# A two-row reload of x on ScalarE's DMA queue, behind the gate's exponential

## The chip, the cores and the metric

The kernel runs on one core of one Trainium2 chip. The metric is the device time of one execution in microseconds, median of several runs. The median before is 137.99 us over three runs (137.84 to 138.12).

## The reference

One decoding step of a transformer block for four tokens (B = 4, D = 1024): grouped-query attention with 32 query heads over 4 key/value heads and a window of the last 2048 cached positions, then a gated feed-forward layer of width 3584. All inputs are bf16.

```python
def _A_ref(x, k_cache, v_cache, wq, wo):
    W = min(4096, max(256, Sk // 4))          # 2048 of 8192 positions
    q = (x @ wq).reshape(B, Sq, Hq, Dh).transpose(0, 2, 1, 3)
    k = jnp.repeat(k_cache[:, :, Sk - W:, :], rep, axis=1)
    v = jnp.repeat(v_cache[:, :, Sk - W:, :], rep, axis=1)
    p = _softmax(jnp.einsum("bhqd,bhkd->bhqk", q, k) * (Dh ** -0.5), axis=-1)
    o = jnp.einsum("bhqk,bhkd->bhqd", p, v)
    return o.transpose(0, 2, 1, 3).reshape(B, Sq, Hq * Dh) @ wo

def _B_ref(x, w1, w3, w2):
    h = _silu(x @ w1) * (x @ w3)
    return h @ w2

h = x + _A_ref(_layernorm(x), A_k_cache, A_v_cache, A_wq, A_wo)
h2 = h + _B_ref(_layernorm(h), B_w1, B_w3, B_w2)      # the output
```

## The kernel before

Some 55.6 MB of weights and cache are read once, and nearly all of the arithmetic is matrix products of a few rows, so the kernel is built around one stream of loads. SyncE (SP) issues it, in the order of the list `plan`, into a ring of SBUF (`ring`, five regions reused in turn): wq in two pieces with two small side loads, k, v, wo, w1, w3, and w2 in four pieces (17, 7, 3 and 1 of its 28 row groups, called w2a to w2d here). `load_next` issues the next entry of the list, and a piece that overwrites a part of the ring waits for the matmuls that read it. All these loads share one DMA queue (q1 in the profile).

ScalarE's own DMA queue (q10) carries three transfers only: two loads at the start that bring x into `x_sb` (L158, four rows of 512 columns each), and the store of the output at the end (L515, sixteen rows of 256 columns). A second copy of x in another layout, `x_q`, comes through SP's queue (L169). `x_sb` is read by the first layernorm alone (L180 and L187) in the first ten microseconds; the tile is kept, and nothing reads it later.

The work after attention goes in stages: `y_ps` (wo, L411), the second layernorm (L424 to L449), `gate_up("w1", g_ps)` on TensorE (L459), and then the gate's SiLU. Of that, ScalarE computes the exponential `eg` (L471), and VectorE adds 1, takes the reciprocal and multiplies by the gate (L472 to L475) while w3 is still arriving. Then `gate_up("w3", u_ps)`, the product `hg` (L478), a transpose, and the `down` products with w2 (L492). VectorE and ScalarE each copy half of the result (L513, L514), and ScalarE issues the store (L515).

Order around the change. The framework puts instructions of each engine in a fixed order and draws the waits itself. Transfers issued by SP and ScalarE get one of eight completion semaphores, in turn in the order of issue, and a transfer first waits until the former user of its semaphore has landed. The kernel before has 24 such transfers, exactly three rounds of eight: the third round is wo, w1, w3, w2a, w2b, w2c, w2d and the store, so the store has the eighth semaphore. At the end of the program (all of it at L541) SP waits for all of these semaphores and for the other engines, with two semaphores per wait instruction, in this order: third and fourth; second and fifth; first and sixth; seventh and VectorE's; eighth and ScalarE's. Then the engines meet at barriers, and the program ends.

`tc.issue_after(ins)` orders what is issued inside its block behind `ins` on the same engine; it does not make it wait until `ins` has finished.

Of the kernel before, what the change touches and what calls it, by code (L numbers as in the profile page):

```python
# [11 lines left out]
ACT = mybir.ActivationFunctionType  # L12
# [7 lines left out]
def kernel(  # L20
# [13 lines left out]
    nc = tc.nc  # L34
# [14 lines left out]
    x_flat = A_x.flatten_outer_dims()  # L49
# [19 lines left out]
    CG = D // JG  # L69
    CF = F // JG  # L70
    HF = CF // 2
# [84 lines left out]
    x_sb = act.tile([B, D], BF16)  # L156
# [11 lines left out]
    for c in range(2):  # L168
        nc.sync.dma_start(  # L169
            out=x_q[c * 2 * QD : (c + 1) * 2 * QD : RS, :],  # L170
            in_=x_flat.rearrange("b (j c) -> j b c", j=JG)[2 * c : 2 * c + 2],
# [7 lines left out]
    for c in range(2):  # L179
# [8 lines left out]
        out=xn[:], in0=x_sb[:], scalar1=mv[:, 0:1], scalar2=rstd[:, 0:1],  # L188
# [14 lines left out]
    for r0, ne, ns in SETS:  # L203
# [3 lines left out]
            out=xs[:, len(sl) : len(sl) + ns, : ne * 4].rearrange("b l (i s) -> b l i s", s=4),  # L207
            in_=v[:, KC - 1, :, :, :],
        )
        for l in range(ns):  # L210
            nc.tensor.transpose(
                out=ts_ps[: ne * 4, len(sl), :], in_=xs[:, len(sl), : ne * 4], identity=ident[:B, :B]
# [4 lines left out]
    for _, ne, ns in SETS:  # L217
# [14 lines left out]
        out=perm[:].rearrange("p (h dq) -> p h dq", dq=JG),  # L232
        in_=ident[:].rearrange("p (dq h) -> p h dq", dq=JG),
# [12 lines left out]
    for j in range(2, JG):  # L246
        nc.vector.tensor_tensor(
            out=same[:, 0, :], in0=same[:, 0, :], in1=ident[:, j * QD : (j + 1) * QD], op=ALU.add
# [35 lines left out]
    for r in range(REP):  # L284
        nc.tensor.transpose(out=qt_ps[:, r, :], in_=q_sb[:, r * Dh : (r + 1) * Dh], identity=ident[:])
    nc.vector.tensor_copy(
        out=qz[:, :, : Hkv * QD].rearrange("p b (g z) -> p b g z", g=Hkv)[:, :, :, :REP],
        in_=qt_ps[:].rearrange("p r (g x) -> p x g r", g=Hkv)[:, :B, :, :],
# [24 lines left out]
    for u, (b, n) in enumerate(units):  # L313
        k_v = loaded["k"][b]
        kT = ktpool.tile([P, NJ, P], BF16, tag="kT")
        for t in range(NJ // TB):
            kt_ps = psA.tile([P, TB, P], BF16, tag=f"kt{nt % 4}")
            for jj in range(TB):
                nc.tensor.transpose(  # L319
                    out=kt_ps[:, jj, :], in_=k_v[:, n * NJ + t * TB + jj, :], identity=ident[:]  # L320
# [21 lines left out]
        out=Pm[:], in_=scores_ps[:], func=ACT.Exp, bias=nmax[:], scale=1.0, accum_out=rsum[:]  # L342
# [6 lines left out]
    for c in range(NSB):  # L349
# [4 lines left out]
        for g in range(Hkv):  # L354
            if g % 2 == 0:
                nc.vector.tensor_scalar(  # L356
                    out=z[:, :, g, :], in0=pt_ps[:], scalar1=mask[:, g : g + 1], scalar2=None, op0=ALU.mult
# [10 lines left out]
        out=Dm[:], in0=ident[:].rearrange("p (g b r) -> p b g r", g=Hkv, b=B),  # L368
# [38 lines left out]
    g_ps = psB.tile([P, 2, 512], FP32, tag="g")  # L407
    u_ps = psB.tile([P, 2, 512], FP32, tag="u")
    for i in range(IO):
# [34 lines left out]
        out=hn[:], in0=h1[:], scalar1=tot[:, 0:1], scalar2=rstd2[:, 0:1],  # L444
# [5 lines left out]
        out=hnT[:].rearrange("p k x -> p (k x)"), in_=hn[:].rearrange("q (c k) -> q k c", k=KC)  # L450
# [3 lines left out]
    def gate_up(kind, out_ps):  # L454
# [13 lines left out]

    gate_up("w1", g_ps)
    eg = wide.tile([P, 2, HF], FP32, tag="w4k")  # L470
    nc.scalar.activation(out=eg[:], in_=g_ps[:, :, :HF], func=ACT.Exp, scale=-1.0)  # L471
    nc.vector.tensor_scalar_add(out=eg[:], in0=eg[:], scalar1=1.0)  # L472
    nc.vector.reciprocal(out=eg[:], in_=eg[:])  # L473
    gs = wide.tile([P, 2, HF], FP32, tag="w4k")
# [7 lines left out]
        out=hgT[:].rearrange("p i x -> p (i x)"),  # L482
        in_=hg[:].rearrange("q s c -> q (s c)").rearrange("q (c i) -> q i c", i=IF),
# [62 lines left out]
```

## Time and profile before

| | |
|---|---|
| median of the runs | 137.99 us (137.84 to 138.12) |
| profiled execution | span 136.0 us from its first to its last instruction; the page gives no other time of it, and the median is 1.99 us above the span |
| busy: PE, DVE, ACT | 72.3, 43.9, 31.0 us |
| DMA queue q1 (SP's loads) | 2604 packets, 55.58 MB, 95.6% of the 16 DMA engines' time |
| DMA queue q10 (ScalarE's) | 36 packets, 0.02 MB, 0.0% |
| mean TensorE clock granted | 0.720 |

The span counts from the first to the last instruction of the program. Issue times of transfers are times of the issuing engine's sequencer; the data moves later, and its landing is told by the completion semaphore. In views of the profile, "SPq" and "ACTq" are the sequencers of SP and ScalarE. Times with three decimals are start times of single records of the trace, in microseconds from the span's start.

### The profile page before, as it was taken

To read this page: it belongs to the slowest core of one execution; us is meant where nothing else is said; L and a number is where in the kernel's file an instruction comes from. 1 tells how busy PE (TensorE), PEld (TensorE's weight loads), DVE (VectorE), ACT (ScalarE), POOL (GpSimd) and SP (SyncE) were. 2 spreads that over 40 slices of the span, in tenths; PEclk is the share of its full clock that TensorE was granted. 3 is DMA by queue.
4 is the path that set the end of the run, shared out by engine and by line. 5 is a ranking of instruction groups with operands and counts; after the bars stand their busy time and mean duration, and the time that the engine had idled before them with its cause. 6 is when DMAs were issued, how large, how long until landed. Compare 5 with 4: busy or idle time off the path is not lost.

```text
span 136.0 us, 2436 instructions
## 1 busy us (share of the span) xinstructions
PE 72.3 (53%) x1096; PEld 46.1 (34%) x1096; DVE 43.9 (32%) x79; ACT 31.0 (23%) x36; POOL 1.7 (1%) x8
## 2 busy tenths in 40 slices
PE   0004920979898989810525916791097000970981
PEld 0002300268374756500014905570043000430870
DVE  5055000043344444470994001206200596026010
ACT  3000000015555555609294300000001400000000
POOL 5000000000000000000000000000000000000000
PEclk9999975557999999985555555568556855568568
DMA  5999999999999999999989999989989899999970
GB/s 155 464 463 406 412 420 414 429 424 439 424 439 424 424 443 426 410 552 453 463 347 463 463 410 405 477 354 494 439 371 494 371 472 401 399 420 407 424 298 5
DMA packets 2650, 55.75 MB, mean 410 GB/s; under 512 B 296, under 2 KB 464, under 8 KB 720
## 3 DMA queue, kind: packets, MB, share of 16 engines
q1 hardware_dynamic: 2604, 55.58, 95.6%
q8 instruction: 8, 0.13, 0.3%
q10 hardware_dynamic: 36, 0.02, 0.0%
q14 instruction: 2, 0.02, 0.0%
HBM read 55.59 MB, written 0.01 MB: 409 GB/s over the span
## 4 chain that ended last, share of the span: by engine, by line
DMA 54%; PE 25%; ACT 11%; DVE 5%; SPq 2%; issue 1%; ACTq 0%
DMA ring<-in_B_w_dram 38%; DMA ring<-in_A_wq_dram 15%; PE kt_ps L319 11%; ACT kT L325 5%; PE scores_ps L304 5%; ACT z L360 3%; PE q_ps L263 3%; DVE rmax L336 2%; ACT Pm L341 2%; PE OT_ps L382 2%; DVE pT L350 1%; SPq L120 1%; PE g_ps L459 1%; DVE z L356 1%; ACT L341 1%
## 5 line engine op out<-in xcount | busy, mean ns | idle before, releaser
L325 ACT COPY kT<-kt_ps 128x1024 bf16<-128x1024 bf16 x16 | 15.9, 1013 | 13.4 <-PE kt_ps L319 13.4
L319 PE MATMUL kt_ps<-ident,ring 128*128 128x128 bf16 x256 | 18.0, 232 | 0.0
L319 PEld LDWEIGHTS <-ring 128*128 128x128 bf16 x256 | 16.0, 105 | 4.9 <-issue 4.9
L323 DVE COPY kT<-kt_ps 128x1024 bf16<-128x1024 bf16 x16 | 11.1, 692 | 16.5 <-PE kt_ps L319 16.5
L459 PEld LDWEIGHTS <-hnT 128*32 128x32 bf16 x128 | 5.5, 143 | 21.8 <-issue 19.2
L382 PE MATMUL OT_ps<-z,ring 128*128 128x32 bf16 x256 | 7.5, 188 | 8.5 <-ACT z L360 5.0
L459 PE MATMUL u_ps<-ring,hnT 128*32 128x448 bf16 x64 | 6.0, 563 | 11.0 <-DMA ring<-in_B_w_dram 11.0
L304 PE MATMUL scores_ps<-kT,qz 128*32 128x512 bf16 x64 | 9.9, 609 | 2.9 <-ACT kT L325 2.9
L263 PE MATMUL q_ps<-ring,xnT 128*4 128x512 bf16 x63 | 6.7, 595 | 7.8 <-DMA ring<-in_A_wq_dram 7.8
L382 PEld LDWEIGHTS <-ring 128*128 128x128 bf16 x256 | 7.4, 104 | 9.2 <-issue 9.2
L459 PE MATMUL g_ps<-ring,hnT 128*32 128x448 bf16 x64 | 5.9, 558 | 4.9 <-DMA ring<-in_B_w_dram 4.9
L492 PEld LDWEIGHTS <-hgT 128*32 128x32 bf16 x156 | 4.9, 134 | 6.2 <-issue 5.7
L411 PE MATMUL y_ps<-ring,o 128*32 128x256 bf16 x128 | 5.9, 371 | 0.8 <-DVE o L398 0.8
L514 ACT CAST res<-yb_ps 128x128 bf16<-128x128 f32 x1 | 0.3, 266 | 26.1 <-PE yb_ps L492 26.1
L492 PE MATMUL y_ps<-ring,hgT 128*32 128x256 bf16 x68 | 3.8, 419 | 4.4 <-DMA ring<-in_B_w_dram 4.4
L360 ACT ACTIVATE z<-pt_ps,mask 128x512 bf16<-128x512 f32 x8 | 5.3, 687 | 3.5 <-DVE z L356 3.5
L352 PE MATMUL pt_ps<-pT,perm 128*128 128x512 bf16 x4 | 2.4, 607 | 6.8 <-DVE pT L350 6.8
L263 PEld LDWEIGHTS <-xnT 128*4 128x4 bf16 x63 | 2.0, 115 | 11.7 <-issue 11.6
L194 PE MATMUL tp_ps<-ident,xn 4*128 4x4 bf16 x8 | 0.7, 200 | 10.0 <-DVE xn L187 10.0
L356 DVE TENSOR_SCALAR z<-pt_ps,mask 128x512 bf16<-128x512 f32 x8 | 5.5, 741 | 1.2 <-ACT z L360 0.8
L473 DVE RECIPROCAL eg<-eg 128x896 f32<-128x896 f32 x1 | 5.8, 5753 | 0.0
L411 PEld LDWEIGHTS <-o 128*32 128x32 bf16 x128 | 4.4, 131 | 3.1 <-DVE o L398 1.9
(85 smaller groups left out, 50.1 us busy)
## 6 DMA issues: line engine op xcount, KB each, us to landing
ring<-in_B_w_dram SPq DMA_DIRECT2D x2, 7168.0 KB, 22.5
ring<-in_A_k_cache_dram SPq DMA_DIRECT2D x4, 2048.0 KB, 27.6
ring<-in_A_v_cache_dram SPq DMA_DIRECT2D x4, 2048.0 KB, 29.2
ring<-in_B_w_dram SPq DMA_DIRECT2D x1, 4352.0 KB
ring<-in_A_wq_dram SPq DMA_DIRECT2D x1, 4096.0 KB, 12.2
ring<-in_A_wq_dram SPq DMA_DIRECT2D x1, 3968.0 KB
ring<-in_B_w_dram SPq DMA_DIRECT2D x1, 1792.0 KB
ring<-in_B_w_dram SPq DMA_DIRECT2D x1, 768.0 KB
```

Of the source, the lines that this page charges most:

```text
L263: nc.tensor.matmul(q_ps[QD * g : QD * g + B, hf * 512 : hf * 512 + n], lhsT=xnT[:, kc, :], rhs=wq_t[:, c0 : c0 + n], start=(kc == 0), stop ...
L304: nc.tensor.matmul(scores_ps[QD * g : QD * (g + 1), n * 512 : (n + 1) * 512], lhsT=qz_v[:, z0 : z0 + QD], rhs=kT_v[:, g, :, :], start=(b = ...
L319: nc.tensor.transpose(out=kt_ps[:, jj, :], in_=k_v[:, n * NJ + t * TB + jj, :], identity=ident[:])
L323: nc.vector.tensor_copy(out=kT[:, t * TB : (t + 1) * TB, :], in_=kt_ps[:])
L325: nc.scalar.copy(out=kT[:, t * TB : (t + 1) * TB, :], in_=kt_ps[:])
L356: nc.vector.tensor_scalar(out=z[:, :, g, :], in0=pt_ps[:], scalar1=mask[:, g : g + 1], scalar2=None, op0=ALU.mult)
L360: nc.scalar.mul(out=z[:, :, g, :], in_=pt_ps[:], mul=mask[:, g : g + 1])
L382: nc.tensor.matmul(OT_ps[:, b, :], lhsT=loaded["v"][b][:, j, :], rhs=PTz[j // NJ][:, (j % NJ) * B + b, :, :], start=(j == 0), stop=(j == J ...
L411: nc.tensor.matmul(y_ps[QD * j : QD * (j + 1), :], lhsT=o4[:, i, :, :].rearrange("p b s -> p (b s)"), rhs=loaded["wo"][i][:, j * CG : (j + ...
L459: nc.tensor.matmul(out_ps[QD * j : QD * (j + 1), hf, :HF], lhsT=hnT[:, k, :], rhs=loaded[kind][k][:, c0 : c0 + HF], start=(k == 0), stop=( ...
L473: nc.vector.reciprocal(out=eg[:], in_=eg[:])
L492: nc.tensor.matmul(out_ps[QD * j : QD * (j + 1), :n], lhsT=hgT[:, i, :], rhs=loaded["w2"][i][:, j * CG + c0 : j * CG + c0 + n], **kw,)
```

## The change

Behind the exponential of the gate, ScalarE issues one more load: rows 0 and 1 of x, columns 0 to 255, into the same place of `x_sb`. The bytes that it writes are those that the tile holds already (1 KB, two rows of 512 bytes). Nothing reads them afterwards.

```diff
     gate_up("w1", g_ps)
     eg = wide.tile([P, 2, HF], FP32, tag="w4k")
-    nc.scalar.activation(out=eg[:], in_=g_ps[:, :, :HF], func=ACT.Exp, scale=-1.0)
+    exp_i = nc.scalar.activation(out=eg[:], in_=g_ps[:, :, :HF], func=ACT.Exp, scale=-1.0)
+    with tc.issue_after(exp_i.ins):
+        nc.scalar.dma_start(out=x_sb[0:2, 0:CG], in_=x_flat[0:2, 0:CG])
     nc.vector.tensor_scalar_add(out=eg[:], in0=eg[:], scalar1=1.0)
     nc.vector.reciprocal(out=eg[:], in_=eg[:])
```

## The prediction

> **What bounds the kernel now.** I read the chain that ended last first, to see whether ScalarE's place in the program is on the path.
>
> ```profile
> DMA 54%; PE 25%; ACT 11%; DVE 5%; SPq 2%; issue 1%; ACTq 0%
> ...
> 100.48 29.74 DMA ring<-in_B_w_dram
> 130.22 0.04 issue
> 130.27 0.30 PE ya_ps L492 x3
> ...
> 132.97 0.09 PE yb_ps L492 x4
> 133.06 0.02 issue
> 133.08 0.27 ACT res L514
> ```
>
> The first line is the page's share of the chain, the others are the chain in order of time (start, length, what). From 76.27 the stream of weights sets the time, up to 130.22; then the last w2 products run, then ScalarE's copy and the store. At 106, where the change goes in, ScalarE's work is not in the chain. Next, ScalarE's own timeline from there (start, length, instruction, and in brackets the idle time before it):
>
> ```profile
> 104.77 1.28 ACT L471 ACT_TABLE_LOAD   x1 [9.93 <-PE g_ps L459]
> 106.06 0.92 ACT L471 ACTIVATE eg<-g_ps 128x896 f32<-128x896 f32 x1
> 133.08 0.27 ACT L514 CAST res<-yb_ps 128x128 bf16<-128x128 f32 x1 [26.10 <-PE yb_ps L492]
> 133.39 0.64 ACTq L515 DMA_DIRECT2D out_dram<-res  x1
> ```
>
> Behind the exponential lie 26.10 us with nothing on ScalarE. Then the issues of small transfers, by line (min/median/max in ns, then first and last start):
>
> ```profile
> L158 ACTq DMA_DIRECT2D x_sb<-in_A_x_dram x2: 265/414/563, 0.7 to 1.3; - x2
> L169 SPq DMA_DIRECT2D x_q<-in_A_x_dram x2: 532/544/557, 14.9 to 23.6; - x2
> L120 SPq DMA_DIRECT2D t<-in_A_wq_dram x2: 801/883/965, 1.2 to 2.2; - x2
> L515 ACTq DMA_DIRECT2D out_dram<-res x1: 639/639/639, 133.4 to 133.4; - x1
> ```
>
> And last the end of the program, what SP does there from 135.1 on, and what it had waited for (us in total, times, longest):
>
> ```profile
> L541 SPq EVENT_SEMAPHORE  x3: 17/17/28, 135.2 to 135.9; - x3
> L541 SPq DRAIN  x3: 7/7/13, 135.2 to 135.6; - x3
> ...
> SPq L541 <- DMA out_dram<-res: 1.8, 1, 1.8
> ```
>
> The store is issued at 133.39, has landed at 135.18, and the closing barriers take the span from there to 136.0. Whatever lengthens those 2.6 us is paid in full.
>
> **The change, part by part.** It removes nothing and moves nothing; it adds one issue on ScalarE, two short packets on two DMA engines, and one more user of the completion semaphores.
>
> *The issue on ScalarE.* Nearest rows: 0.265 us for the second x load (four rows, plain), 0.639 us for the store (sixteen rows, two-level pattern). Two plain rows are nearest to the first: 0.27. Before it stand waits for the former writers of the tile and the former user of its semaphore; all of these landed before 63 us (the v loads are the latest), so each costs one short step, 0.05 to 0.06 us by SP's rows below. Everything lies in the 26.10 us of idle time, and behind it on ScalarE is only the copy at 133.08, which waits for TensorE. On the path: 0. If it slipped ahead of the exponential, it would push VectorE's three steps by at most 0.64; they end at 114.6, and their reader L478 stood idle for 7.09 us waiting for `u_ps`. Still 0. A gain is excluded here: no work goes away.
>
> *The packets in the stream.* The reload has a packet of 512 bytes and a 4-byte semaphore packet on each of two engines. The row for it is x_q: it too runs on two engines, four packets of 512 bytes and a semaphore packet on each, in the middle of the stream at 52.1 to 52.3, and its packets follow each other by 24 ns, the semaphore packet taking 5 to 9, so 0.10 us for the five and 0.03 us for the reload's two. What happens when another queue cuts in shows at the second x load: its 1 KB packet starts at 6.122, lasts 46 ns, and SP's next 32 KB packet begins on that engine at 6.164; the semaphore packet comes at 7.376 and the next 32 KB one at 7.382. No gap opens. So two of the 16 engines are put back by 0.03 us. Eleven engines finish w3 between 114.84 and 115.34 and five a good microsecond earlier (113.57 to 114.19), so that only if one of the two is the last to finish does it count: 0 to 0.03 us, I take 0.01. The reload's packets queue behind descriptors of 57,344 bytes (2.116 us each), so by the second x load, which came to its data 4.5 us after its issue and to its semaphore one 32 KB packet later, it lands by about 115 us. Nobody waits for it before SP's closing waits.
>
> The Trainium skill ("DMA: Bandwidth & Descriptors", Queues, rings and completion order) says that an engine drains a whole packet of about 9 to 17 descriptors from one queue before it turns to the next; the trace shows the turn after single packets, and by the rule the reload would land later, but still before the store, with the same sum.
>
> *The end.* This is the only place where I find a cost. The reload is the 24th transfer and takes the eighth semaphore; the store becomes the 25th and takes the first. SP's closing waits have a fixed order. Before, the pair with the store's semaphore was the last of five, and at 135.181 SP passed from it straight to its drain at 135.246. Now the store's semaphore is in the third pair: SP stands there until the store has landed and then still has two wait instructions to go through, both satisfied. A satisfied wait and the step to the next one took 0.053 us at 76.647 (to 76.700), 0.054 at 100.861 (to the issue at 100.915) and 0.065 at 135.181. Two of them: 0.11 to 0.13, I take 0.12. This is behind the last landing, so nothing hides it. Bounds: 0, if the order of the pairs follows the store after all, and 0.26 (four steps), if its pair comes first.
>
> *The store itself.* A recent use of ScalarE's queue could make the store's issue quicker. For it: the first x load on ScalarE took 0.563 us and the second, of the same shape, 0.265, a difference of 0.298. Against it: the store's 0.639 is already what a queue in use gives. x_q has 8 packets in 0.544 and the second load of L120 has 48 in 0.801; in a straight line 16 packets take 0.544 + 8 x 0.257/40 = 0.595, so at most 0.04 is left. SP's issues do not grow with idle time either: 0.338 for wo at 42.79, and 0.334 for w1 33 us later. From the end of the store's issue (134.03) to its first packet (134.66) it takes 0.63, while the first x load, the first use that queue ever had, took 0.40 (1.305 to 1.702): an unused queue is not slow in that row. And the first x load ran beside SP's first issue (0.732 to 1.109), while the second ran alone for most of its time. Bounds for this part: 0 to -0.30, and -0.53 if the 0.23 go too. I take 0, since SP's rows after idle time are nearest.
>
> The skill ("Perfetto Trace Analysis", DMA Instruction — HWDGE) has the shown length of an issue include the wait for a descriptor generator that two sequencers share; by that the 0.298 is a wait behind SP's issue and nothing can be won at the store (138.1), where a cold start would give 137.8.
>
> **Sum.** On the profiled span: 136.0 + 0 + 0.01 + 0.12 + 0 = 136.13. The median stands 1.99 above the span, and nothing that the change does lies there: 137.99 + 0.13 = 138.12, so 138.1 us. That is under 0.1%; a difference under 0.2% (0.28 us) is about what a measurement of this kernel can't tell from no change.
>
> **Rivals.**
>
> *The queue is woken for the store.* The store's issue falls from 0.639 to about 0.34, as from the first x load to the second. With the two closing steps: 137.99 - 0.30 + 0.13 = 137.8; with the 0.23 before its first packet too, 137.6. For it speaks only the pair of x loads; the straight line through SP's rows speaks against it, and the store would still come 27 us after the reload.
>
> *The reload costs the stream real time (slower).* Two engines are held not for 0.03 us but for the length of a foreign transfer. The instruction fetches on queue 8 hold one engine for 0.88 to 0.97 us per 16 KB. If the switch to the other queue cost as much as such a fetch, w3 on that engine would end 0.9 us later; w3 and w2 follow back to back, so all of it reaches the end: 137.99 + 0.9 + 0.12 = 139.0. It decides as soon as one of the two engines is among the eleven late ones and loses over about 0.16 us. The second x load, which left no gap, speaks against it.
>
> *It does not do what it says:* the reload is issued early, or the semaphores are dealt in an order that leaves the store in the last pair. Then there is no closing cost: 138.0.
>
> **How the numbers follow.** Forecast 0.66, woken queue 0.14, stream 0.12, not as said 0.08. Of the forecast's 0.66, 0.56 stays within the bound, 0.09 goes over it (the closing cost at its upper end and scatter) and 0.01 under. The woken queue gives 0.09 faster and 0.05 same, the stream 0.12 slower, the last rival 0.07 same and 0.01 slower. Together 0.10 faster, 0.68 same, 0.22 slower. The range goes down to 137.75, which takes in the woken issue but not the further 0.23, and up to 138.5, which takes in the closing cost of 0.26, the scatter of the runs (0.13 up) and the small end of the stream's case; its large end and the strongest wakening stay outside, with some 0.15 to 0.2.
>
> **What would show it.** Right: one ScalarE issue of about 0.27 us at 106 to 107.5; two packets of 512 bytes on q10 before 116; `u_ps` starting at 115.7 and the copy L514 at 133.1 as before; a store issue near 0.64; and SP's closing waits with two more short ones after the store's landing, 0.12 us later to the end. Wrong: a store issue near 0.35 (the queue was woken), or w3 and w2 landing later by tenths (the stream paid), or the same number of waits after the landing (no closing cost).

## The result and the profile after

The changed kernel takes 138.42 us (138.35 to 138.56, five runs) where the kernel before takes 137.99 beside it; the ratio is 1.0038, 95% interval 1.0028 to 1.0049. So it is slower by 0.43 us, more than the 0.28 us that the prediction took for no change. The forecast was 138.1, with a chance of 0.68 on no change and 0.22 on slower. The measured median lies inside the stated range, but on the side that had the smaller chance.

The chain that ended last, in the changed kernel: first the page's shares, then, from the chain in order of time, its end (start, length, what).

```profile
DMA 53%; PE 25%; ACT 11%; DVE 5%; SPq 2%; issue 1%; ACTq 0%
```

```profile
100.50 29.78 DMA ring<-in_B_w_dram
...
133.01 0.08 PE yb_ps L494 x4
133.10 0.02 issue
133.12 0.27 ACT res L516
```

The stream of weights ends as before (100.50 + 29.78 = 130.28, before 130.22), and ScalarE's last copy starts 0.04 us later. Up to there next to nothing has happened. ScalarE's timeline from the exponential on, in the changed kernel:

```profile
104.70 1.28 ACT L471 ACT_TABLE_LOAD   x1 [9.92 <-PE g_ps L459]
104.82 0.24 ACTq L473 DMA_DIRECT2D x_sb<-in_A_x_dram  x1
105.99 0.92 ACT L471 ACTIVATE eg<-g_ps 128x896 f32<-128x896 f32 x1
133.12 0.27 ACT L516 CAST res<-yb_ps 128x128 bf16<-128x128 f32 x1 [26.21 <-PE yb_ps L494]
133.77 0.63 ACTq L517 DMA_DIRECT2D out_dram<-res  x1
```

Two things are to be seen. The reload is issued at 104.82, while the table for the exponential is still loading: the sequencer hands the exponential on and goes to the next instruction. And the store starts 0.65 us after the copy, where before it started 0.31 after it (133.08 and 133.39). What lies between is one wait of ScalarE's, for VectorE's half of the result. The store's line in the changed kernel, and SP's closing instructions from 135.3 on (times of one in ns, min/median/max, first and last start):

```profile
L517 ACTq EVENT_SEMAPHORE  x1: 266/266/266, 133.1 to 133.1; - x1
L517 ACTq DMA_DIRECT2D out_dram<-res x1: 634/634/634, 133.8 to 133.8; - x1
```

```profile
L543 SPq EVENT_SEMAPHORE  x5: 17/28/5288, 130.3 to 136.4; - x5
L543 SPq DRAIN  x3: 7/7/13, 135.7 to 136.1; - x3
```

The wait is as long as before (266 ns) and ends at 133.391; the store's issue begins at 133.774. Before, these two were at 133.351 and 133.389. A pause of 0.383 us stands where there were 0.038, and no wait of the program accounts for it: ScalarE's own semaphore, the store's only remaining condition, came at 133.394. At the end SP now stands in its third pair of waits until the store has landed (the 5288 ns), and goes through two more waits, at 135.615 and 135.676, before its drain at 135.741.

The span grew by 0.496 us (136.495 against 135.999), and the records split it without a rest: copy and wait end 0.040 later (133.391 against 133.351), the pause is 0.345 longer, issue to last landing takes 0.007 more (1.782 against 1.775), from there to SP's drain it takes 0.103 more (0.185 against 0.082), and the barriers 0.001.

### The profile page after: what moved, and what is told of

It reads as the page before. It is cut to its first block, busy times and chain, and to the rows that moved or that the text cites. A ratio compares the mean times of both kernels' runs of the same rounds, so it can differ in the third digit from the quotient of the medians.

```text
span 136.5 us, 2438 instructions
## 1 busy us (share of the span) xinstructions
PE 74.1 (54%) x1096; PEld 46.3 (34%) x1096; DVE 44.0 (32%) x79; ACT 31.0 (23%) x36; POOL 1.7 (1%) x8
## 4 chain that ended last, share of the span: by engine, by line
DMA 53%; PE 25%; ACT 11%; DVE 5%; SPq 2%; issue 1%; ACTq 0%
DMA ring<-in_B_w_dram 38%; DMA ring<-in_A_wq_dram 15%; PE kt_ps L319 10%; ACT kT L325 5%; PE scores_ps L304 5%; ACT z L360 3%; PE q_ps L263 3%; DVE rmax L336 2%; ACT Pm L341 2%; PE OT_ps L382 1%; DVE pT L350 1%; SPq L120 1%; PE g_ps L459 1%; DVE z L356 1%; ACT L341 1%
## 5 line engine op out<-in xcount | busy, mean ns | idle before, releaser
L263 PE MATMUL q_ps<-ring,xnT 128*4 128x512 bf16 x63 | 7.2, 626 | 5.5 <-DMA ring<-in_A_wq_dram 5.5
L360 ACT ACTIVATE z<-pt_ps,mask 128x512 bf16<-128x512 f32 x8 | 5.3, 688 | 3.5 <-DVE z L356 3.5
L281 DVE TENSOR_SCALAR q_sb<-q_ps 128x512 bf16<-128x512 f32 x1 | 0.7, 692 | 14.6 <-PE q_ps L263 14.6
```

What stands on the lines that cost most here:

```text
L263: nc.tensor.matmul(q_ps[QD * g : QD * g + B, hf * 512 : hf * 512 + n], lhsT=xnT[:, kc, :], rhs=wq_t[:, c0 : c0 + n], start=(kc == 0), stop ...
L360: nc.scalar.mul(out=z[:, :, g, :], in_=pt_ps[:], mul=mask[:, g : g + 1])
```

## The experiments

The closing waits were in the prediction; the pause was not. Three theories of it. **Place**: the pause belongs to a place in ScalarE's program. The reload and the wait ahead of it add two instructions, so that the store moves from the 62nd to the 64th. **Queue**: an earlier use of ScalarE's DMA queue slows the next. **Semaphore**: the store now has the first completion semaphore instead of the eighth. The profile's list of DMA queues gave the place theory a handle; in the changed kernel it has

```profile
q8 instruction: 8, 0.13, 0.3%
q10 hardware_dynamic: 40, 0.02, 0.1%
q14 instruction: 2, 0.02, 0.0%
```

Queue 14 carries two packets of 8192 bytes in the span. In the kernel before, the later one starts at 135.65; in the changed kernel at 134.41, 0.64 us after the pause. All the kernels below were run five times or more beside the kernel before. The diffs leave out the lines around the edit and those that only set up a tile or a name.

**e1: two copies in place of the reload.**

```diff
-        nc.scalar.dma_start(out=x_sb[0:2, 0:CG], in_=x_flat[0:2, 0:CG])
+        for c in range(2):
+            nc.scalar.copy(out=scr[:, c : c + 1], in_=rsum[:])
```

> No reload; instead ScalarE does two one-column copies into a scratch tile behind the exponential, so that the store is again the 64th instruction of ScalarE's program (62nd before, 64th in the changed kernel) and keeps the eighth semaphore. Place theory (the pause of 0.38 us between ScalarE's last wait and the store's issue comes from where the store stands in ScalarE's instruction order): the pause is there, 0.38 instead of 0.04, no closing cost, about 138.3. Queue theory (it comes from the reload on ScalarE's DMA queue) and semaphore theory (it comes from the store using the first semaphore instead of the eighth): pause 0.04, about 138.0.

Measured: 138.40 against 137.93, ratio 1.0035 (1.0024 to 1.0047). ScalarE's end in this kernel:

```profile
133.35 0.27 ACT L518 CAST res<-yb_ps 128x128 bf16<-128x128 f32 x1 [25.88 <-PE yb_ps L496]
134.01 0.64 ACTq L519 DMA_DIRECT2D out_dram<-res  x1
```

Copy to store is 0.66 us, the pause 0.387 (133.621 to 134.008), the 8 KB packet at 134.65. There is no reload, no further use of ScalarE's queue, and the store has its eighth semaphore: the queue and semaphore theories fall. The longer pause is 0.349 us of the 0.48 that the ratio stands for; the interval (0.33 to 0.65) takes it in.

**e2: the reload issued by SP, behind its last weight load** (`last[0]` is the last transfer that `load_rows` issued).

```diff
+    with tc.issue_after(last[0].ins):
+        nc.sync.dma_start(out=x_sb[0:2, 0:CG], in_=x_flat[0:2, 0:CG])
```

> The reload is issued by SP behind its last weight load, so ScalarE's program is that of before (store 62nd), while the store gets the first semaphore as in the changed kernel. Place theory: pause 0.04, closing cost of two waits 0.10 to 0.12, about 138.1. Queue theory: the same, 138.1. Semaphore theory: pause 0.38 and closing cost, about 138.4.

Measured: 137.98 against 137.93, ratio 1.0008 (0.9999 to 1.0017), so 0.11 us with an interval that reaches zero. ScalarE's end in this kernel:

```profile
133.27 0.27 ACT L517 CAST res<-yb_ps 128x128 bf16<-128x128 f32 x1 [26.75 <-PE yb_ps L495]
133.58 0.64 ACTq L518 DMA_DIRECT2D out_dram<-res  x1
```

and SP's closing waits, of which the one of 3231 ns ends with the store's landing:

```profile
L544 SPq EVENT_SEMAPHORE  x5: 17/28/3231, 132.1 to 136.2; - x5
```

The store has the first semaphore and follows its copy after 0.31 us, as before the change; SP's two extra waits are there (135.410, 135.472, drain at 135.537).

**e3: the reload on ScalarE, behind the softmax's exponential** (the two added lines moved up to L341).

> ScalarE issues the reload some 40 us earlier, behind the softmax's exponential (L341); the store is the 64th instruction and has the first semaphore, as in the changed kernel. Place theory and semaphore theory: pause 0.38 and closing cost, about 138.4. Queue theory: 138.4 if any earlier use of the queue does it, 138.1 with a pause of 0.04 if only a use late in the program does.

Measured: 138.51 against 137.93, ratio 1.0045 (1.0032 to 1.0059); pause 0.380, packet at 134.37, SP's two extra waits behind the landing. When the reload is issued does not matter.

**e4: the changed kernel with four copies behind the reload.**

> The changed kernel with four one-column copies on ScalarE behind the reload: the store is the 68th instruction, semaphores as in the changed kernel. Place theory: the pause leaves the store (0.04), the closing cost stays, about 138.1; if the place that pauses lies just behind the store's old one, the pause falls into ScalarE's idle time and costs nothing. Queue theory and semaphore theory: pause 0.38, about 138.4.

Measured: 138.44 against 137.93, ratio 1.0042 (1.0030 to 1.0055). The pause was gone (0.038), as the place theory had it, and yet the time was not: a miss by 0.3 us. The stream shows why. How long TensorE stood waiting for w3 in the changed kernel, and then in this one (us in total, times, longest):

```profile
PE u_ps L459 <- DMA ring<-in_B_w_dram: 11.2, 1, 11.2
```

```profile
PE u_ps L459 <- DMA ring<-in_B_w_dram: 12.3, 1, 12.3
```

`u_ps` starts at 116.53, where it started at 115.76 in the changed kernel. The 8 KB packet of queue 14 now starts at 109.145, in the middle of w3, by its time right behind one of the reload's packets on the same engine (109.122; such packets follow each other by 24 ns). One engine finishes w3 at 116.04, the others by 115.38 (this is the slowest of the five runs, 138.72). ScalarE's 64th instruction is now one of the copies, which starts at 106.57 instead of 133.77, and the packet has moved into the stream with it. What it costs its engine can be read there: it lasts 0.309 us, and the 57,344-byte load packet right behind it, at 109.451, lasts 2.361 us, where such packets last 2.116. Together that is 0.55 us. The reload's own packets hold an engine for 0.024 us, and the load packet behind one of them (109.041) lasts its 2.116.

**e5: the changed kernel, with x brought in by one load at the start instead of two.** ScalarE's program loses one instruction, and the transfers are 24 again, so that the store is back on the eighth semaphore.

```diff
-    for c in range(2):
-        nc.scalar.dma_start(out=x_sb[:, c * 512 : (c + 1) * 512], in_=x_flat[:, c * 512 : (c + 1) * 512])
+    nc.scalar.dma_start(out=x_sb[:], in_=x_flat[:, :])
```

> The changed kernel with x brought into x_sb by one load at the start instead of two: ScalarE's program is one instruction shorter (the store is the 63rd), and the transfers are 24 again, so that the store is back on the eighth semaphore and in SP's last closing pair; the reload is issued as in the changed kernel. Place theory with the closing cost: no pause (0.04) and one step after the landing as before, so all of the loss is gone, 137.9 to 138.0, with the reload still there. If the reload itself costs (queue theory, or the stream), 138.1 or more.

Measured: 137.89 against 137.92, ratio 1.0002 (0.9994 to 1.0011). The reload is there (issued at 103.99) and costs nothing. ScalarE's end in this kernel, and then its closing drain by line:

```profile
133.09 0.27 ACT L515 CAST res<-yb_ps 128x128 bf16<-128x128 f32 x1 [27.01 <-PE yb_ps L493]
133.40 0.63 ACTq L516 DMA_DIRECT2D out_dram<-res  x1
```

```profile
L542 ACTq DRAIN  x1: 237/237/237, 134.4 to 134.4; - x1
```

The store follows at once. The pause has moved behind it: the issue ends at 134.037 and the drain starts at 134.426, 0.389 us later, where before the change it was 0.040. There ScalarE has nothing to do but wait for the store to land.

**e6: the kernel before with one copy.** The store is the 63rd.

> Kernel before with one one-column copy on ScalarE behind the exponential: the store is the 63rd instruction, eighth semaphore. Place theory with the pause at the 64th instruction: no pause at the store (0.04), about 138.0; the pause then falls behind the store, where ScalarE has nothing to do. If the boundary lies at the 63rd, or any shift of the store does it: 0.38, about 138.3.

Measured: 137.89 against 137.92, ratio 1.0005 (0.9996 to 1.0014). ScalarE's end in this kernel, and then its closing drain:

```profile
133.17 0.27 ACT L518 CAST res<-yb_ps 128x128 bf16<-128x128 f32 x1 [26.86 <-PE yb_ps L496]
133.48 0.64 ACTq L519 DMA_DIRECT2D out_dram<-res  x1
```

```profile
L545 ACTq DRAIN  x1: 241/241/241, 134.5 to 134.5; - x1
```

No pause at the store (0.038); 0.386 behind it. One added instruction is free, two put 0.35 us ahead of the store.

**e7 and e8: the kernel before with three and with four copies** (store 65th and 66th).

> Kernel before with three copies: the store is the 65th instruction, and the 64th is ScalarE's wait for VectorE's half of the result, which starts with its own copy of 0.27 us and ends with it. Place theory: a pause of 0.35 before that wait, of which 0.27 lies beside the copy, so that the store is issued 0.08 to 0.12 later than before relative to the copy's end: 138.0 to 138.1; the fetch still after 133. Queue and semaphore theories: 138.0.

> Kernel before with four copies and no reload: the 64th instruction is ScalarE's last copy (L514), which ScalarE's sequencer reaches at about 107 and where it waits for TensorE. Place theory: no pause at the store (0.04); the 8 KB fetch on queue 14 goes out at about 107 to 110, among the w3 loads, and puts one DMA engine back by 0.3 us or more. If that engine is one of the late ones, w3 lands 0.3 to 0.7 later and all after it: 138.2 to 138.5; if it is one of the five early ones, 137.9 to 138.0. No closing cost.

Measured: e7 138.33 against 137.92, ratio 1.0035 (1.0022 to 1.0047); e8 138.27 against 137.92, ratio 1.0031 (1.0019 to 1.0042). For e7 the expectation (138.0 to 138.1) missed by 0.2 us and was wrong in its mechanism: no pause shows ahead of the last wait, and the packet does not come after 133 but at 108.91, among the w3 loads, as in e8 (108.87). With ScalarE's last copy as the 63rd instruction, the packet goes out while that copy still waits for TensorE. In both kernels the engine that took the packet can be followed, since each load packet starts where the one before it ends: the load packet behind it lasts 2.366 us instead of 2.116, two more of 2.116 follow, and then comes the packet with which that engine closes w3, at 115.80 in e7 and 115.77 in e8. It is the last of the 16 engines in both. The start of `u_ps` in the changed kernel, in e8 and in e9 (min/median/max in ns, first to last start):

```profile
L459 PE MATMUL u_ps<-ring,hnT x64: 353/581/581, 115.8 to 121.3; 128*32 128x448 bf16 x64
```

```profile
L459 PE MATMUL u_ps<-ring,hnT x64: 352/577/581, 116.2 to 121.4; 128*32 128x448 bf16 x64
```

```profile
L463 PE MATMUL u_ps<-ring,hnT x64: 424/577/581, 116.1 to 121.7; 128*32 128x448 bf16 x64
```

**e9: the kernel before with sixteen copies in ScalarE's idle stretch behind L360.**

> Kernel before with sixteen one-column copies on ScalarE in its idle stretch from 75 to 94 us (behind its last attention product L360): ScalarE's 64th instruction is one of these copies, so that the pause lies in idle time and the 8 KB fetch goes out at about 76 to 80, while wo and w1 arrive; the store is the 78th, eighth semaphore. No pause at the store, no closing cost. If a fetch in the stream costs wherever it falls, the loads from there on land 0.3 to 0.6 later: 138.2 to 138.5. If the stream has slack there, 137.9 to 138.0.

Measured: 138.28 against 137.87, ratio 1.0031 (1.0020 to 1.0043). The packet starts at 76.50, half a program earlier, and `u_ps` is again late, at 116.1. The load packet behind it lasts 2.660 us instead of 2.418. Its engine is then the last to finish wo, at 81.87 (the last in the kernel before: 81.52), and w1, at 98.78 (98.43), and w3 ends at 115.69 (115.34): 0.35 us late each time. So the fetch costs about the same at 76 as at 109: what one engine loses while the stream is the bound is not won back. In this kernel and in e4 the 63rd and 64th instructions are copies, and they start 0.093 and 0.094 us apart, as their neighbours do: no pause shows on the engine itself there.

**e10: four reloads on SP**, so that the store has the fourth semaphore, which is in the first closing pair.

> Kernel before with four reloads of the changed kernel's size issued by SP behind its last weight load: ScalarE's program is that of before (no pause), the store gets the fourth semaphore, which is in the first of SP's five closing pairs. Closing cost by the changed kernel's profile, 0.06 per wait: four waits more after the landing, 0.24 to 0.26, about 138.2. If the order of the closing waits did not matter: 137.95.

Measured: 138.23 against 137.87, ratio 1.0026 (1.0016 to 1.0035). SP's closing instructions:

```profile
L545 SPq EVENT_SEMAPHORE  x7: 17/28/28, 135.4 to 136.4; - x7
L545 SPq DRAIN  x3: 7/7/13, 135.7 to 136.0; - x3
```

Five of the waits start one after another after the landing, at 135.411, 135.475, 135.542, 135.607 and 135.668, and the drain at 135.733: four steps more than before, 0.26 us together.

Put side by side (the place counts ScalarE's instructions with its waits; the waits after the landing are SP's wait instructions that end after the store has landed; times in us):

| kernel | place of the store | pause | 8 KB packet | last engine done with w3 | waits after the landing | ratio |
|---|---|---|---|---|---|---|
| before | 62 | 0.038 | 135.65 | 115.34 | 1 | 1 |
| changed | 64 | 0.383 | 134.41 | 115.39 | 3 | 1.0038 |
| e1 | 64 | 0.387 | 134.65 | 115.45 | 1 | 1.0035 |
| e2 | 62 | 0.039 | 135.85 | 115.39 | 3 | 1.0008 |
| e3 | 64 | 0.380 | 134.37 | 115.32 | 3 | 1.0045 |
| e4 | 68 | 0.038 | 109.15 | 116.04 | 3 | 1.0042 |
| e5 | 63 | 0.039 | 135.20 | 115.27 | 1 | 1.0002 |
| e6 | 63 | 0.038 | 135.53 | 115.44 | 1 | 1.0005 |
| e7 | 65 | 0.039 | 108.91 | 115.80 | 1 | 1.0035 |
| e8 | 66 | 0.039 | 108.87 | 115.77 | 1 | 1.0031 |
| e9 | 78 | 0.039 | 76.50 | 115.69 | 1 | 1.0031 |
| e10 | 62 | 0.039 | 135.87 | 115.50 | 5 | 1.0026 |

Every kernel whose store is at the 64th place has the pause; every kernel whose packet falls into the stream has one engine late with w3; and those with neither and one wait after the landing run like the kernel before. In the eight kernels whose packet comes at the end, it starts 1.02 to 1.42 us after ScalarE's 63rd instruction has ended; in e10 that is 0.09 us before the 64th begins (135.87 and 135.96).

## Why the prediction was wrong

*The issue on ScalarE* was put at 0, because 26 us of idle time hide it. The issue itself is hidden (0.238 us, near the 0.27 taken). The step failed in what else an added instruction does: it moves all that follow it in the program. The reload is two instructions, a wait and the issue, and they carry the store over a boundary at which ScalarE's sequencer stops for 0.38 us. Nothing covers that, since the store is the last work of the program. This is the missing term: 0.345 us of the 0.496 in the span. That 138.42 still lies in the range up to 138.5 is luck, since the range was opened for other causes: the closing cost, the scatter and a little of the stream's case. That idle time hides a duration, and not a place in the program, was nowhere in the sum.

*The store itself* was bounded from one side only, 0 to -0.53: I asked whether its issue could become quicker and never what could delay it. The argument against a gain held: the issue took 0.634 us, before 0.639, and 0.634 in e5 with the reload ahead of it. The rival of the woken queue is out.

*The end* was right in mechanism and nearly in size: 0.12 forecast, 0.103 in the changed kernel's records, 0.11 (-0.01 to 0.23) by the times of e2. Its bound of 0.26 for four steps is what e10's records show (by e10's times 0.36, with an interval of 0.22 to 0.48).

*The stream* was right for the reload: two packets on queue 10 at 109.01 and 109.02, landed at 111.48 (I had said by 115), w3 done at 115.39 against 115.34, and e5 shows the reload at no cost. The rival's price of a foreign transfer was not idle, though: the fetch of 8 KB takes 0.55 us from its engine, and the last engine is done with w3 0.35 to 0.46 us later where it falls into the stream (e7 to e9; 0.70 in e4's profiled run). It was just not the reload that sent it.

*Not as forecast, without consequence:* the reload was issued at 104.82 and not after 106, and in the order of issue it came between w3 and w2a, so that it took the fourth semaphore, not the eighth, and the w2 loads moved on by one. The store still got the first.

What stays open. That the pause is part of fetching instructions is argued from the packet, which the profile files under "instruction" and which follows ScalarE's 63rd and 64th instructions through all twelve kernels; where there is a pause, the packet starts 0.64 to 1.03 us after it is over, so the pause is not the time of its bytes. Why no pause shows in e4, e7, e8 and e9 is open too; in those the 63rd instruction is a copy, where in the five with the pause it is a wait or an issue of the sequencer's. In the kernel before, e2 and e10 the boundary falls among the closing drains and waits, and there no pause can be told from waiting. The Trainium skill ("Runtime: NRT & Kernel Launch", Instruction fetch mechanics) has each engine refill its instruction memory in blocks of 16 KiB over a DMA queue of its sequencer's own, and calls the cost of crossing a block mostly hidden. The packets here are of 8 KB, and the crossing is hidden only where the engine has time: at the store the pause cost 0.345 us, and in the stream the packet cost about as much.

## What to carry to other kernels

An instruction that is free by its duration still shifts everything behind it on its engine; near the end of a program, look in the trace for pauses that no wait explains and for the packets on the "instruction" queues, and count on which side of such a boundary the last instructions stand. One instruction less elsewhere on the engine can take the whole cost away (e5: one load instead of two, which also gave the store its old semaphore back). A transfer added anywhere also turns the deal of completion semaphores, and the last transfer of the program should be in the last wait that the program closes with: each closing wait behind its landing costs 0.05 to 0.07 us.

## What the runs showed of the hardware

- A pause of 0.380 to 0.389 us in ScalarE's instruction order ahead of its 64th instruction, in five kernels, where neighbouring steps take 0.04 (at the store in the changed kernel, e1 and e3; behind it in e5 and e6). Where the 63rd is a copy (e4, e7, e8, e9), none shows.
- An 8 KB packet on queue 14 lasts 0.309 us in the stream, and the load packet behind it takes 0.24 to 0.25 us longer than others of its size (e4, e7, e8, e9), so that one DMA engine loses 0.55 us. It becomes the last one (w3 done at 115.69 to 116.04 against 115.27 to 115.50), and the kernel is slower by a ratio of 1.0031 to 1.0035 (e7 to e9), whether the packet falls at 76 or at 109.
- ScalarE's sequencer issues a transfer placed behind an exponential before the exponential starts: 104.82 against 105.99.
